# Attention's transposes moved from VectorE to the DMA engines, and the down/wo weight sums from VectorE to accumulating DMAs in DRAM

## The chip, the cores and the metric

The kernel runs on one core of one Trainium2 chip. Times are device microseconds (us). PE is TensorE, DVE is VectorE, ACT is ScalarE, POOL is GpSimd, SP is SyncE, which issues most of the DMAs. PEld is TensorE's loading of weights. A name with a q at the end (SPq, POOLq) is that engine's queue of instructions, which keeps the order that the program gave it. L335 is line 335 of that run's own kernel, so the same operation has other numbers in other runs. In an operation `out<-in` names the tiles; in a list of waits `a <- b` means that a waited for b.

## The reference, cut to what matters

```python
# x: 1 x 2048 x 1024 (bf16), wqkv: 1024 x 3072, wo: 1024 x 1024, w_gate and w_up: 1024 x 3584, w_down: 3584 x 1024
g = sigmoid((x * gate_w).sum(-1, keepdims=True))
a = attention(x @ wqkv) @ wo          # 32 heads of 32; each query sees 8 keys, at distances 0, 2, .. 14
b = (gelu(x @ w_gate) * (x @ w_up)) @ w_down
return g * a + (1 - g) * b
```

## The kernel before: the parts that matter

The 2,048 rows are handled as four chunks of 512. The gate/up products run twice (two passes of two chunks, 14 blocks of weights each), the down and wo products once per chunk. These products are done with seven half-size matrix products in place of eight, which needs sums and differences of weight blocks ("forms"). A program in Python lays out all instructions beforehand: every piece of work is an `Op` with an assumed cost, and the order on each engine is fixed by those costs. On the chip each engine then follows its fixed order and waits where data is late.

Three parts matter here. First, the forms of the gate/up weights. In the first pass they are made by VectorE from four loaded pieces and stored to DRAM from GpSimd's queue for the second pass. Pieces and forms live in a ring of 20 slots, and a form's slot is only free again when TensorE has used it **and** its store has landed:

```python
def wforms():                                   # per block of gate/up weights: four forms
    ...
    o = dve(t, go, [("w", 0, b, x_), ("w", 0, b, y_)], key=("w", 0, b, f), lag=0.5, pre=ring_pre)
    yield o
    ...
    yield Op("POOL", (P * GR * 2, 0.6),
             lambda b=b, f=f: nc.gpsimd.dma_start(out=fdram[b][:, f * GR:(f + 1) * GR], in_=ring[:, held[("w", 0, b, f)], :]),
             [("w", 0, b, f)], key=("ws", b, f))
# in the gate/up products, first pass, when a form has been used:
ring_give(("w", sup, b, form), o, w.done[("ws", b, form)])      # o: the matmul, ws: the store
```

Second, the forms of the down and wo weights. They are staged in SBUF, summed by VectorE and stored, all but one store of them before the gate/up pass begins at 93 us:

```python
def preps():                                    # nine steps
    f0 = dve(t, lambda: V(out=fo[:, 0], in0=b12, in1=b11, op=ALU.subtract), [("prep", i0)], lag=1.0)
    ...                                         # four such differences, then four 256 KB stores
    o = Op("POOL", ..., lambda f=f: nc.gpsimd.dma_start(out=dd[:, f, r0:r0 + n, :], in_=fo[:, f]), [last], ...)
```

Third, attention, in eight halves of a chunk. The products of queries and keys are turned by VectorE in blocks of 32 x 32, and the weights are turned back later:

```python
o = dve(2.24, taking("z", lambda: nc.vector.transpose(out=flat("z"), in_=xbuf[:, accs[h], :])), [("qk", h)], ...)
...
def back(i=i):
    nc.vector.transpose(out=flat("ab")[:, i * n // 2:(i + 1) * n // 2], in_=flat("e")[:, i * n // 2:(i + 1) * n // 2])
```

## Time and profile before

| | before |
|---|---|
| median, 3 runs | 733.29 us (732.34 to 733.42) |
| PE busy | 721.8 of 729.7 us (99%) |
| VectorE busy | 631.6 us (87%) |
| share of the 16 DMA engines, 8 to 50 us / 141 to 200 us | 1.09 / 0.72 |

Lines of the profile's page for the kernel before: span, busy time by engine, busy tenths in 40 equal slices, and the DMA queues (q1 is fed by SyncE, q0 by GpSimd; ScalarE has a queue of its own, q10, with 0.2%; the last figure is the share of the 16 engines' time).

```profile
span 729.7 us, 9971 instructions
...
PE 721.8 (99%) x3397; PEld 356.0 (49%) x3397; DVE 631.6 (87%) x935; ACT 314.9 (43%) x532; POOL 72.0 (10%) x128
...
PE   8999999999999999999999998999999999999998
...
DVE  2689999999999989999899999999999999969300
...
DMA  9999965648892869943029999555455544899992
...
q1 hardware_dynamic: 142624, 135.30, 60.1%
q0 software_dynamic: 8544, 27.27, 10.1%
```

TensorE is never idle for a slice. Here is whom it waited for, from the list of waits of before (total us, times, longest):

```profile
PE ps L970 <- ACT m L1024: 2.1, 1, 2.1
PE ps L279 <- DVE hT L277: 1.2, 1, 1.2
PE ps L1212 <- DMA hT<-in_A_x_dram: 0.8, 1, 0.8
```

So TensorE loses 4.1 us to waits in the whole program. VectorE is busy but not in its way.

### The profile page before, as it was taken

What the parts mean: (1) busy time and instruction counts of PE and PEld (TensorE: products, weight loads), DVE (VectorE), ACT (ScalarE), POOL (GpSimd) and SP (SyncE); (2) the same over time, 40 slices, a digit from 0 to 9 for tenths busy, and PEclk for the clock granted to TensorE, in tenths of its full rate; (3) what the DMA queues carried; (4) which work ended last, traced back from release to release, by engine and by line L of the source; (5) the groups of instructions that cost most, each with busy time, mean ns of one, the idle gap of its engine ahead of it and who ended that gap; (6) DMA issues with size and microseconds to landing.
All of it is one profiled execution on the core that took longest, in us unless ns stands there. A gap on an engine that the chain in (4) does not pass through costs nothing.

```text
span 729.7 us, 9971 instructions
## 1 busy us (share of the span) xinstructions
PE 721.8 (99%) x3397; PEld 356.0 (49%) x3397; DVE 631.6 (87%) x935; ACT 314.9 (43%) x532; POOL 72.0 (10%) x128
## 2 busy tenths in 40 slices
PE   8999999999999999999999998999999999999998
PEld 5666644444444444456665444444444444444443
DVE  2689999999999989999899999999999999969300
ACT  2333455558555561035652113576557654220110
POOL 2234422121210100000000001000000000001000
PEclk9999999999999999999999999999999999999999
DMA  9999965648892869943029999555455544899992
GB/s 302 333 325 363 380 200 170 187 139 212 213 227 74 280 194 326 314 162 116 29 89 300 358 302 333 165 150 155 147 159 147 156 151 145 303 304 336 323 303 104
DMA packets 151507, 163.73 MB, mean 224 GB/s; under 512 B 22944, under 2 KB 112032, under 8 KB 151456
## 3 DMA queue, kind: packets, MB, share of 16 engines
q1 hardware_dynamic: 142624, 135.30, 60.1%
q0 software_dynamic: 8544, 27.27, 10.1%
q8 instruction: 26, 0.43, 0.2%
q10 hardware_dynamic: 288, 0.52, 0.2%
q14 instruction: 25, 0.20, 0.1%
HBM read 129.50 MB, written 28.31 MB: 216 GB/s over the span
## 4 chain that ended last, share of the span: by engine, by line
PE 73%; issue 21%; DVE 2%; ACT 1%; DMA 1%; POOL 1%; POOLq 0%; ACTq 0%
PE ps L970 44%; PE ps L1117 17%; PE ps L473 11%; DVE xbuf L922 1%; POOL out_dram L1144 1%; DMA hT<-in_A_x_dram 0%; DVE xbuf L930 0%; PE ps L1212 0%; DMA out_dram<-ost 0%; DVE xbuf L935 0%; DVE ost L1191 0%; ACT ost L1152 0%; ACT L1058 0%; DVE xbuf L787 0%; PE ps L717 0%
## 5 line engine op out<-in xcount | busy, mean ns | idle before, releaser
L970 PEld LDWEIGHTS <-ring 128*128 128x128 bf16 x1568 | 153.2, 98 | 187.7 <-issue 3.5
L970 PE MATMUL ps<-lend,ring 128*128 128x512 bf16 x896 | 212.3, 379 | 2.2 <-ACT m L1024 2.1
L970 PE MATMUL ps<-tf,ring 128*128 128x512 bf16 x672 | 164.0, 379 | 0.0
L1117 PE MATMUL ps<-ring,hT 128*128 128x512 bf16 x708 | 160.7, 379 | 0.0
L1117 PEld LDWEIGHTS <-hT 128*128 128x128 bf16 x708 | 69.2, 98 | 83.3
L781 DVE TENSOR_TENSOR xbuf<-qo,lend 128x2048 bf16<-128x2048 bf16 x64 | 77.4, 1218 | 2.1 <-ACT lend L495 2.1
L922 DVE TENSOR_TENSOR xbuf<-xbuf,lend 128x2048 bf16<-128x2048 bf16 x64 | 77.4, 1218 | 0.1
L787 DVE TENSOR_TENSOR xbuf<-xbuf 128x2048 bf16<-128x2048 bf16 x56 | 68.2, 1218 | 0.2
L609 PEld LDWEIGHTS <-ring 128*128 128x128 bf16 x336 | 44.0, 131 | 28.7 <-DMA ring<-in_A_wqkv_dram 0.4
L473 PE MATMUL ps<-lend,ring 128*128 128x512 bf16 x256 | 56.3, 381 | 0.1
L1042 ACT ACTIVATE gl<-ps 128x512 bf16<-128x512 f32 x56 | 33.5, 598 | 51.5 <-PE ps L970 51.4
L999 ACT COPY ps<-ps 128x512 f32<-128x512 f32 x56 | 32.0, 571 | 54.9 <-PE ps L970 54.8
L1152 ACT ACTIVATE ost<-ps,omg 128x512 bf16<-128x512 f32 x16 | 11.0, 688 | 102.5 <-PE ps L1117 99.3
L1144 POOL DMA_DIRECT2D out_dram<-ost x24 | 13.0, 540 | 413.4 <-ACT ost L1152 319.4
L1117 PE MATMUL ps<-ring,qo 128*128 128x512 bf16 x192 | 49.3, 379 | 0.0
L473 PEld LDWEIGHTS <-ring 128*128 128x128 bf16 x256 | 36.8, 145 | 19.0 <-issue 0.7
L443 POOL DMA_DIRECT2D fforms<-ring x56 | 30.4, 544 | 132.4 <-DVE ring L435 120.6
L609 PE MATMUL ps<-lend,ring 128*128 128x512 bf16 x192 | 43.5, 379 | 0.0
L1014 DVE TENSOR_TENSOR hT<-hT,gl 128x1024 bf16<-128x1024 bf16 x56 | 38.4, 686 | 5.8 <-ACT hT L1011 4.5
L930 DVE TENSOR_TENSOR xbuf<-xbuf 128x1024 bf16<-128x1024 bf16 x64 | 41.9, 686 | 0.7
L1054 DVE TENSOR_TENSOR u<-ps,u 128x512 f32<-128x512 f32 x56 | 38.4, 686 | 4.6 <-PE ps L970 3.4
L1033 DVE TENSOR_TENSOR hT<-ps,m 128x512 bf16<-128x512 f32 x56 | 38.4, 686 | 4.0 <-PE ps L970 3.9
(106 smaller groups left out, 724.7 us busy)
## 6 DMA issues: line engine op xcount, KB each, us to landing
ring<-dforms SPq DMA_DIRECT2D x112, 256.0 KB, 4.9
ring<-in_B_w_down_dram SPq DMA_DIRECT2D x84, 256.0 KB, 4.1
ring<-in_B_w_gate_dram SPq DMA_DIRECT2D x56, 256.0 KB, 4.7
fforms<-ring POOLq DMA_DIRECT2D x56, 256.0 KB, 4.5
ring<-fforms SPq DMA_DIRECT2D x56, 256.0 KB, 3.9
ring<-in_B_w_up_dram SPq DMA_DIRECT2D x42, 256.0 KB, 3.3
ring<-in_A_wqkv_dram SPq DMA_DIRECT2D x40, 256.0 KB, 4.9
ring<-oforms SPq DMA_DIRECT2D x32, 256.0 KB, 5.6
```

Source lines behind the costliest of these rows:

```text
L473: nc.tensor.matmul(banks[bk][:], lhsT=lhsT, rhs=xT(c, kt), start=(kt == 0), stop=(kt == KT - 1))
L609: nc.tensor.matmul(banks[bk][:], lhsT=lhsT, rhs=rhs[:, kt, :], start=(start and kt == 0), stop=(kt == KH - 1), skip_group_check=True)
L781: V(out=w3(box[t]), in0=q_b, in1=k_w, op=ALU.mult)
L787: V(out=w3(box[0]), in0=w3(box[0]), in1=w3(box[t]), op=ALU.add)
L922: return dve(tt(n), taking(("p", t), lambda: V(out=w3(box["p", t]), in0=w3(box["ab"]), in1=v_w, op=ALU.mult)), [("qkv", c, 2, t), abo] + ( ...
L930: V(out=s4(t)[:, t % 2], in0=w3(box["p", t])[:, 0:4], in1=w3(box["p", t])[:, 4:8], op=ALU.add)
L970: nc.tensor.matmul(banks[bk][:], lhsT=wv[:, k, fl * P:(fl + 1) * P], rhs=rhs[:, k, :], start=(start and k == 0), stop=(k == KH - 1), skip_ ...
L1014: yield dve(tt(2 * SC), lambda f=f: nc.vector.tensor_tensor(out=hT[:, :, f, :], in0=hT[:, :, f, :], in1=gl[f][:].rearrange("p (j s) -> p j ...
L1033: ev[f, "up2"] = dve(tt(SC, True), lambda f=f: nc.vector.tensor_tensor(out=hs(f, 1), in0=v3(banks[Bk[f]][:]), in1=v3(m5[f][:]), op=ALU.add ...
L1042: nc.scalar.activation(out=gl[f][:, SC:2 * SC], in_=banks[A[f]][:], func=ACT.Gelu_apprx_tanh)
L1054: e = dve(tt(SC, True), lambda f=f: nc.vector.tensor_tensor(out=u2[f][:], in0=banks[Dk[f]][:], in1=u2[f][:], op=ALU.add), [o, ev[f, "u2"]])
L1117: nc.tensor.matmul(banks[bk][:], lhsT=l, rhs=wv[:, i, :], start=(start and k == 0), stop=(q == last and i == 1), skip_group_check=True)
```

## The change

The intent is to take about 65 us of work off VectorE and have it done by DMAs. 24 DMA transposes issued from SyncE replace the 24 VectorE transposes, and the sums of the down/wo weights become 64 DMAs from DRAM to DRAM issued from GpSimd, 32 of them accumulating. The accumulating DMAs used here only add, so some signs change further on (`S1` is now a difference, and so on). The loads of x for the second pass become a stream of their own. The core of the diff:

```diff
-        for i0 in range(0, NPREP, 2):
-            ...                                  # staged loads, four VectorE differences, four stores
+        def part(kind, k0, n):
+            ...
+            return [(src(0, 0), dst(0), None), (src(1, 1), dst(2), None), (src(1, 1), dst(1), None), (src(1, 0), dst(3), None),
+                    (src(0, 1), dst(0), ALU.add), (src(0, 1), dst(2), ALU.add), (dst(0), dst(1), ALU.add),
+                    (dst(1), dst(3), ALU.add)]
+        done, j = [("qkv", 0, 1, NT - 1)] * NFLY, 0          # NFLY = 2
+        for kind, k0, n in PARTS:                            # one part of wo (512 KB DMAs), seven of down (256 KB)
+            for src, dst, op in part(kind, k0, n):
+                def go(src=src, dst=dst, op=op):
+                    if op is None:
+                        nc.gpsimd.dma_start(out=dst, in_=src)
+                    else:
+                        nc.gpsimd.dma_start(out=dst, in_=src, accum_op=op, max_dma_last_dim=1024)
+                d = [done[-NFLY]]
+                if j >= NEARLY:                              # NEARLY = 28, PER = 3
+                    d.append(("w", 0, (j - NEARLY) // PER, 3))
+                o = Op("POOL", (n * P * NW * 2 * (2 if op else 1), 1.0), go, d, after=True)
 ...
-        o = dve(2.24, taking("z", lambda: nc.vector.transpose(out=flat("z"), in_=xbuf[:, accs[h], :])), [("qk", h)],
-                pre=xb_pre(), key=("acct", h))
+        def turn(cols, fn, deps, **kw):
+            return Op("SP", (P * cols * 2, max(1.3, cols / 1000.0)), fn, deps, tail=2.0 if h == 0 else 1.1, lag=1.0, **kw)
+        o = turn(n, taking("z", lambda: nc.sync.dma_start_transpose(out=rows("z"), in_=xbuf[:, accs[h], :])), [("qk", h)],
+                 pre=xb_pre(), key=("acct", h))
 ...
-                nc.vector.transpose(out=flat("ab")[:, i * n // 2:(i + 1) * n // 2],
-                                    in_=flat("e")[:, i * n // 2:(i + 1) * n // 2])
+                nc.sync.dma_start_transpose(out=rows("ab")[:, i * NWIN:(i + 1) * NWIN],
+                                            in_=flat("e")[:, i * n // 2:(i + 1) * n // 2])
```

Waits between sums that touch the same bytes are needed for the result; the limit of two sums in flight is the schedule's own choice. The Trainium skill, "DMA: Bandwidth & Descriptors" (Rules for kernel authors), says that an accumulate reads its destination and writes it later with nothing holding the bytes in between, and that one must wait for the earlier DMA's semaphore.

## The prediction

> **What bounds the kernel.** TensorE. The page's first part has PE busy 721.8 of 729.7 us (99%), clock 1.0 in every slice. The groups and timeline show one 128x512 matmul every 0.216 us; the 3,296 of the program need 712 us. The list of waits gives PE only 2.1 us on ScalarE near 456 us, 2.0 us at the start, and some 3.5 us of tail after the last matmul. VectorE is at 87%, but PE hardly waits for it. The DMA engines are saturated from 8 to 93 us (share 1.07) and the down products (0.89 to 0.99 from 275 to 320 us), half free (0.55) in the first gate/up pass.
>
> **What the change moves.** PE's work is unchanged, so nothing below about 727 us is possible.
> - VectorE loses 36 weight sums (0.685 us each, 24.7 us) and the 32x32 transposes (8 of 2.31 us, 16 of 1.23 us: 38.2 us) and small copies: about 65 of 632 us, nearly all off the critical path. At most the 2.1 us wait goes.
> - The sums become 64 DRAM-to-DRAM DMAs from GpSimd, half accumulating. The 36 staged loads and 36 stores (18.9 MB) go. The Trainium skill, "Collectives: The Full Stack" (bandwidth ceiling: AG, RS, AR), says an accumulate is slow because it needs two source reads. No run here shows that yet. Estimate from it: some 27 MB-equivalents, half of it in the gate/up pass.
> - 24 SBUF-to-SBUF DMA transposes (8 MB). The 16 x transposes between 177 and 213 us raise the DMA share by about 0.43 (15.5 us for 2 MB), so an estimate of 3.8 us of all engines per 512 KB and 62 us in total. In the gate/up pass the share goes from 0.55 to about 1.0.
>
> **Where it can hurt.**
> 1. The chain of sums: each waits for the one two before it. Its stores landed in 6.1 us (dforms) and 4.5 us (fforms). Estimate 5 to 6 us for a plain part, 7 to 8 for an accumulate: 64 x 6.5 / 2 = 208 us from about 50 us, ending near 258 us. The first summed weights are needed at about 265 us. So it just makes it, or is late by tens of us.
> 2. The fforms stores of the gate/up forms stand in the same GpSimd queue behind these waits. A late store holds a ring slot and delays the weight loads. There is some 30 us of slack.
> 3. Transposes wait in SyncE's queue while weight loads stand behind them. In the down products (0.87 us per piece, about 10 pieces ahead, landing 4.9 us) only 4 to 5 us are spare, and two halves of the attention fall in each of the stretches 270 to 320 and 400 to 440. I expect a few us of PE waits on ring DMAs there.
>
> **Prediction.** Either nothing is seen (730 to 738 us) or the chain is late and PE waits 15 to 40 us between 110 and 275 us. Median 739 us, range 730 to 772. Faster by over 2%: 0.01; within 2%: 0.58; slower: 0.41.
>
> **What would show it.** VectorE busy near 567 us. PE busy unchanged at 722 us. Accumulates landing later than plain parts, 7 to 8 us. The last dforms DMA issued between 225 and 265 us; if later, a PE wait on a ring<-dforms DMA just after 260 us. GpSimd's waits for sums appear ahead of fforms. Small PE waits for ring loads in the down products of chunks 0 and 1. Transposes land in 5 to 8 us.
>
> **What would make it wrong.** Accumulates far slower than a plain store (over 10 us): then the first pass is bound by the chain and the time goes over 780 us. Or accumulates as quick as plain ones: then 731 us.

## More of the kernel before

The windows of before, in the first gate/up pass and the start of the first down products; the first column is the stretch, then its length, busy time per engine, granted clock, DMA share and GB/s:

```profile
141.00:200.00 59.00, 58.98 (x274) 26.68 (x273) 57.56 (x83) 37.44 (x64) 10.80 (x20) 1.00 0.72 192
200.00:250.00 50.00, 50.00 (x234) 22.66 (x232) 47.84 (x66) 27.79 (x50) 6.49 (x12) 1.00 0.67 180
250.00:300.00 50.00, 50.00 (x233) 22.64 (x232) 46.92 (x71) 18.19 (x28) 1.62 (x3) 1.00 0.81 268
```

The DMA engines have room in these stretches (0.67 to 0.81).

## The result, and the profile after

The changed kernel took **763.64 us** (median of 4 runs, 760.4 to 769.96) against 732.82 us before (4 runs): a ratio of 1.0431, 95% interval 1.0351 to 1.0512. It is slower by over 4%. (Ratios here and below are the mean time of one kernel's fast runs over that of the other's of the same rounds, so not quite the ratio of the medians quoted.) The result is correct.

The same lines of the page, for the changed kernel:

```profile
span 765.1 us, 9884 instructions
...
PE 730.1 (95%) x3397; PEld 357.1 (47%) x3397; DVE 569.9 (74%) x842; ACT 313.9 (41%) x533; POOL 107.1 (14%) x156
...
PE   8999999968988859999999999999999999999998
...
DVE  1898799576877939938979897888999995694201
...
DMA  9797999999999994998212999997566656899993
...
q1 hardware_dynamic: 166368, 134.25, 61.9%
q0 software_dynamic: 18208, 36.71, 20.2%
```

VectorE did get its relief, 569.9 us in place of 631.6. TensorE has gaps from the ninth to the fifteenth slice, that is 153 to 287 us, the later part of the first gate/up pass. GpSimd's DMA queue q0 takes twice its share. TensorE's two large waits, from the list of waits of the changed kernel:

```profile
PE ps L964 <- DVE hT L1027: 15.9, 5, 9.5
PE ps L964 <- ACT m L1018: 13.0, 8, 3.4
```

And its windows, with columns as before:

```profile
141.00:200.00 59.00, 47.82 (x205) 20.52 (x204) 38.27 (x55) 22.79 (x42) 25.36 (x34) 0.94 0.90 219
200.00:250.00 50.00, 43.77 (x192) 18.93 (x191) 40.34 (x59) 23.62 (x44) 20.44 (x31) 0.97 1.14 258
250.00:300.00 50.00, 38.24 (x169) 16.70 (x167) 35.77 (x54) 23.81 (x41) 9.56 (x14) 0.90 0.97 219
```

The two large waits make 28.9 us, where before there was one of 2.1 us. PE's busy time also grew, by 8.3 us (730.1 against 721.8), for the same 3,397 matmuls. The granted clock in the windows tells why: 0.94, 0.97 and 0.90 in place of 1.00. The sum, 26.8 + 8.3 = 35.1 us, is nearly all of the difference of the two spans (765.1 - 729.7 = 35.4 us). The Trainium skill, "TensorE: Matmul & The Clock Gate" (Part 1), has it that the clock falls to half after an idle window of about 3.4 us and needs about as long to recover. This trace agrees in the main: after waits of 3.44 and 9.52 us (both below) the next eight matmuls took 3.57 and 3.39 us, where eight take 1.89 us at full clock, and full clock was back 5.9 and 3.0 us after they started. The limit is not sharp here: after one wait of 2.78 us eight matmuls took 3.23 us, after another of 2.84 us they took 1.89 us.

### One stall, followed back

A stretch of the timeline of the changed kernel: start, duration, engine, line, operation; in brackets the idle time before it and what ended it.

```profile
180.95 3.37 SPq L335 DMA_DIRECT2D ring<-in_B_w_gate_dram  x2
...
182.09 0.69 DVE L424 TENSOR_TENSOR ring<-ring 128x1024 bf16<-128x1024 bf16 x1 [4.71 <-DMA ring<-in_B_w_up_dram]
...
183.76 0.68 DVE L1048 TENSOR_TENSOR u<-ps,u 128x512 f32<-128x512 f32 x1
...
184.48 0.63 ACT L1052 ACTIVATE gl<-u 128x512 bf16<-128x512 f32 x1 [5.45 <-DVE u L1048]
...
185.48 0.59 ACT L1018 COPY m<-ps 128x512 f32<-128x512 f32 x1
...
186.12 3.57 PE L964 MATMUL ps<-lend,ring 128*128 128x512 bf16 x8 [3.44 <-ACT m L1018]
```

Read it from the bottom. TensorE idled 3.44 us for a ScalarE copy (L1018). ScalarE had to do the gelu (L1052) first in its order, and that waited 5.45 us for a VectorE add (L1048). VectorE had to make a weight form (L424) first in its order, and that waited 4.71 us for a weight piece that was late. Nothing here is short of engine time: one late load stops three in-order queues in turn.

Why was the load late? These are SyncE's own waits for stores of forms in the changed kernel, between 140 and 200 us and then over the whole run:

```profile
SPq L335 <- DMA fforms<-ring: 51.8, 11, 9.6
...
SPq L335 <- DMA fforms<-ring: 72.8, 17, 9.6
```

For 51.8 of 60 us SyncE stood before a weight load (L335) because the ring slot was still held by a store of a form (fforms<-ring). Before the change no such line exists. The stores were not slow to land once issued (5.2 to 8.6 us in this stretch); they were issued late, since they stand behind the sums in GpSimd's queue. GpSimd's waits for sums in the changed kernel:

```profile
POOL dforms L406 <- DMA dforms<-dforms: 41.1, 7, 7.6
POOL dforms L406 <- DMA dforms<-in_B_w_down_dram: 36.0, 15, 5.1
...
POOL dforms L404 <- DMA dforms<-in_B_w_down_dram: 23.4, 11, 5.1
...
POOL dforms L404 <- DMA dforms<-dforms: 16.1, 6, 4.5
```

These are 116.6 us of standing still in that queue. The line of 41.1 us holds a wait that the schedule did not foresee: it counts on two sums in flight, but the last accumulate of a part reads what the one just before it writes.

TensorE's longest wait, 9.5 of the 28.9 us, has another cause. It does not come from a weight load; what it goes back to is a DMA transpose (L907):

```profile
263.61 7.27 SPq L907 DMA_TRANSPOSE xbuf<-xbuf  x2
...
265.49 4.26 POOL L432 DMA_DIRECT2D fforms<-ring  x7
...
282.04 1.23 DVE L916 TENSOR_TENSOR xbuf<-xbuf,lend 128x2048 bf16<-128x2048 bf16 x1 [12.36 <-DMA xbuf<-xbuf]
...
283.79 0.68 DVE L1027 TENSOR_TENSOR hT<-ps,m 128x512 bf16<-128x512 f32 x1
...
284.52 3.39 PE L964 MATMUL ps<-tf,ring 128*128 128x512 bf16 x8 [9.52 <-DVE hT L1027]
```

VectorE stood 12.36 us before its attention work until the transpose had landed, and behind it in its order stood the operation (L1027) that TensorE needed. The transposes L907 took 5.6 us to land in the median, these two 17.3 and 14.1 us. While these two were being issued, GpSimd began to issue seven held-back stores in a row (256 KB each, from 265.5 us); that these delayed the transpose is a guess that no run tried.

### The profile page after: what moved, and what is told of

The parts are those of the page before. It is cut to its first block, busy times and chain, and to the rows that moved or that the text cites. A ratio compares the mean times of both kernels' runs of the same rounds, so it can differ in the third digit from the quotient of the medians.

```text
span 765.1 us, 9884 instructions
## 1 busy us (share of the span) xinstructions
PE 730.1 (95%) x3397; PEld 357.1 (47%) x3397; DVE 569.9 (74%) x842; ACT 313.9 (41%) x533; POOL 107.1 (14%) x156
## 3 DMA queue, kind: packets, MB, share of 16 engines
q0 software_dynamic: 18208, 36.71, 20.2%
## 4 chain that ended last, share of the span: by engine, by line
PE 68%; DMA 21%; issue 4%; DVE 2%; POOL 2%; ACT 2%; SPq 0%; POOLq 0%; DVEq 0%; ACTq 0%
PE ps L1111 28%; PE ps L964 26%; PE ps L598 9%; DMA dforms<-in_B_w_down_dram 6%; DMA dforms<-dforms 4%; PE ps L462 4%; DMA oforms<-in_A_wo_dram 2%; DMA ring<-in_B_w_up_dram 2%; DMA xbuf<-xbuf 2%; DMA oforms<-oforms 2%; DMA ring<-in_B_w_gate_dram 2%; POOL dforms L404 1%; DMA fforms<-ring 1%; DMA ring<-in_A_wo_dram 1%; POOL fforms L432 1%
## 5 line engine op out<-in xcount | busy, mean ns | idle before, releaser
L964 PEld LDWEIGHTS <-ring 128*128 128x128 bf16 x1568 | 154.5, 99 | 222.0 <-issue 42.8
L964 PE MATMUL ps<-lend,ring 128*128 128x512 bf16 x896 | 215.5, 383 | 13.2 <-ACT m L1018 13.0
L964 PE MATMUL ps<-tf,ring 128*128 128x512 bf16 x672 | 166.7, 384 | 16.1 <-DVE hT L1027 15.9
L1052 ACT ACTIVATE gl<-u 128x512 bf16<-128x512 f32 x56 | 35.4, 632 | 60.1 <-DVE u L1048 60.0
L424 DVE TENSOR_TENSOR ring<-ring 128x1024 bf16<-128x1024 bf16 x56 | 38.1, 687 | 29.4 <-DMA ring<-in_B_w_up_dram 18.0
L1048 DVE TENSOR_TENSOR u<-ps,u 128x512 f32<-128x512 f32 x56 | 38.4, 686 | 6.6 <-PE ps L964 6.0
```

Source lines behind the costliest of these rows:

```text
L424: nc.vector.tensor_tensor(out=g, in0=ring[:, held[("w", 0, b, x_)], :], in1=ring[:, held[("w", 0, b, y_)], :], op=op)
L964: nc.tensor.matmul(banks[bk][:], lhsT=wv[:, k, fl * P:(fl + 1) * P], rhs=rhs[:, k, :], start=(start and k == 0), stop=(k == KH - 1), skip_ ...
L1048: e = dve(tt(SC, True), lambda f=f: nc.vector.tensor_tensor(out=u2[f][:], in0=banks[Dk[f]][:], in1=u2[f][:], op=ALU.add), [o, ev[f, "u2"]])
L1052: ev[f, "g2"] = act(0.54, lambda f=f: nc.scalar.activation(out=gl[f][:, 0:SC], in_=u2[f][:], func=ACT.Gelu_apprx_tanh), [e], table="gelu")
```

## The experiments

Theories. **Queue**: sums stand in front of the stores in GpSimd's queue, slots come free late, weight loads come late. **Traffic**: the sums and transposes fill the DMA engines (share 0.90 to 1.14 between 141 and 250 us, where before it was about 0.7), and everything lands late, whoever issues it. **Transposes**: a late DMA transpose holds the in-order queues of VectorE or SyncE.

| label | what it is | median us | ratio to before | 95% interval |
|---|---|---|---|---|
| (changed kernel) | | 763.64 | 1.0431 | 1.0351 to 1.0512 |
| e1_dve_turns | sums by DMA, transposes on VectorE | 750.32 | 1.0248 | 1.0221 to 1.0276 |
| e2_dve_sums | transposes by DMA, sums on VectorE | 733.70 | 1.0019 | 0.9977 to 1.0060 |
| e3_stores_act | changed, stores of forms from ScalarE | 749.32 | 1.0229 | 1.0201 to 1.0258 |
| e4b_half | changed, sums move half the bytes (wrong result) | 733.61 | 1.0011 | 0.9981 to 1.0042 |
| e5_turns_stores | e1 and e3 together | 736.40 | 1.0055 | 1.0030 to 1.0080 |
| e6_plain | changed, no accumulating (wrong result) | 740.96 | 1.0118 | 1.0079 to 1.0157 |
| e7_pairs | changed, two parts interleaved | 753.48 | 1.0289 | 1.0245 to 1.0333 |
| e8_pairs_stores | e7 and e3 together | 751.50 | 1.0264 | 1.0246 to 1.0281 |
| e9_patient | e3, later landing of transposes foreseen | 752.95 | 1.0295 | 1.0273 to 1.0318 |
| e10_traffic | e5 and unused copies from SyncE | 741.62 | 1.0135 | 1.0115 to 1.0155 |
| e11_many | e10 with the copies cut in 128 KB DMAs | 753.54 | 1.0299 | 1.0253 to 1.0345 |

All but the two marked gave correct results. The kernel before had medians of 731.98 to 732.82 us in these rounds.

### Each half of the change alone: e1_dve_turns and e2_dve_sums

```diff
# e1: in the changed kernel, the transposes as before (and with them the layout of the gate's sums)
-        o = turn(n, taking("z", lambda: nc.sync.dma_start_transpose(...
+        o = dve(2.24, taking("z", lambda: nc.vector.transpose(...
# e2: in the changed kernel, load_prep() and preps() as before, with the new signs
-                        nc.gpsimd.dma_start(out=dst, in_=src, accum_op=op, max_dma_last_dim=1024)
+            f0 = dve(t, lambda: V(out=fo[:, 0], in0=b12, in1=b11, op=ALU.add), [("prep", i0)], lag=1.0)
```

> Undoes one half: the attention's transposes are back on VectorE as before, the accumulating sums stay. Queue theory (sums stand ahead of the forms' stores in GpSimd's queue, late stores hold ring slots, weight loads come late): most of the loss stays, 748 to 760 us, and SyncE's queue still waits over 40 us for the fforms stores. Transpose theory (a late DMA transpose holds VectorE's or SyncE's in-order queue): most of the loss goes, 733 to 740 us.

> Undoes the other half: the sums are back on VectorE with staged loads and stores, the DMA transposes stay. Queue theory: 732 to 740 us, no wait of SyncE's queue for fforms stores, PE waits under 6 us. Transpose theory: most of the loss stays, 750 us or more, with VectorE waiting for xbuf<-xbuf transposes.

The DMA transposes alone cost nothing that these runs can tell (1.0019, interval across 1), and VectorE waited 8.7 us for them in e2, where it waited 27.9 us in the changed kernel. The sums alone cost 2.5%. SyncE's wait for stores in e1, in its own queue's list:

```profile
SPq L336 <- DMA fforms<-ring: 66.8, 12, 14.7
```

That is close to the 72.8 us of the changed kernel. The transposes by themselves are out as the cause. But the two halves do not add up: 18 us and 2 us alone, 31 us together. Something that the sums do makes the transposes harmful.

### Taking the stores out from behind the sums: e3_stores_act and e5_turns_stores

```diff
-             lambda b=b, f=f: nc.gpsimd.dma_start(out=fdram[b]...
+             lambda b=b, f=f: nc.scalar.dma_start(out=fdram[b]...
```

The laying out of the program is left as it was, so TensorE, VectorE and SyncE keep their order.

> The changed kernel with the 56 stores of the gate/up forms issued from ScalarE instead of GpSimd; the order on PE, VectorE and SyncE is the same, the DMA work too. Queue theory: the stores land soon after their sums, SyncE's wait for fforms stores (72.8 us) falls below 20 us, time 738 to 750 us. Bandwidth theory (the DMA engines are full, whoever issues): no change, 757 to 768 us.

> Transposes back on VectorE (as e1_dve_turns, 750.3 us) and the forms' stores issued from ScalarE (as e3_stores_act, 749.3 us): only the accumulating sums are left on GpSimd, alone in its queue. If the sums alone hurt by their place ahead of the stores: 732 to 737 us. If they hurt by filling the DMA engines even without the transposes' traffic: 742 to 750 us.

SyncE's wait for stores fell from 72.8 us to 0.4 us in e3. Its only line for stores there:

```profile
SPq L907 <- DMA fforms<-ring: 0.4, 1, 0.4
```

The edit also moves the stores to another kind of DMA queue (q10, a hardware queue). That they land sooner once issued is not the reason: their median landing is 7.2 us in e3 and 7.7 us in the changed kernel. The time fell by 14.3 us in e3 (763.64 to 749.32) and by 13.9 us in e5 (750.32 to 736.40). The same edit is worth the same with and without the DMA transposes, so the queue part is shown, and it is some 14 of 31 us. This is what moving the stores was worth in all, for they now stand in ScalarE's order: at 228.0 and 238.6 us in e3 TensorE waited 2.95 and 2.85 us for a ScalarE copy that stood behind such a store. It is the larger part of what the sums cost alone (18 us). TensorE's waits in e5:

```profile
PE ps L961 <- ACT ps L990: 2.7, 3, 1.2
PE ps L961 <- ACT m L1015: 1.9, 2, 1.0
...
PE ps L961 <- ACT u L1041: 0.8, 1, 0.8
```

Some 0.55% (4 us) is left in e5, and 2.3% (17 us) in e3. The expected range for e3 (738 to 750 us) was met only just, at its upper end; the queue theory is not the whole.

e5 also answers the traffic theory in its plain form. Its windows, beside 0.90 and 1.14 in the changed kernel:

```profile
141.00:200.00 59.00, 59.00 (x275) 26.70 (x273) 54.80 (x78) 32.01 (x59) 14.80 (x16) 1.00 0.97 245
200.00:250.00 50.00, 46.28 (x212) 20.55 (x211) 45.15 (x72) 29.19 (x52) 9.93 (x11) 1.00 1.17 267
```

The DMA engines are as full as in the changed kernel, and the loss is 4 us.

### What a sum costs: e4b_half and e6_plain

```diff
# e4b: half of the rows of each part, and the loads of the forms read only what was written
-                return B_w_down[r0:r0 + n * P, ...]
+                return B_w_down[r0:r0 + n // HALF * P, ...]
# e6
-                        nc.gpsimd.dma_start(out=dst, in_=src, accum_op=op, max_dma_last_dim=1024)
+                        nc.gpsimd.dma_start(out=dst, in_=src)
```

> Wrong result on purpose: each of the 64 DMAs of the sums moves half its bytes, with the same number, order and waits. Bandwidth theory: the sums' DMA load halves, most of the loss goes, 735 to 747 us. Queue theory: a sum's latency is mostly fixed (5.8 us for 256 KB[...]), so the chain is hardly shorter: 750 to 762 us.

> Wrong result on purpose: the 32 accumulating DMAs are plain copies of the same bytes; orders on all engines unchanged. If the second read and the adding make the sums dear: these land in about 5.3 us (plain ones in the changed kernel) instead of 7.1 us, the software queue's share of the DMA engines falls from 20% to about 16%, time 738 to 752 us. If accumulating costs little: 757 to 768 us.

Half the bytes took away the whole loss, where I had expected the queue's part to stay: a miss. I had taken a sum's latency as mostly fixed. It was not: the median landing of accumulates fell from 7.2 to 5.3 us, that of the plain parts from 5.3 to 4.4, the last sum was issued at 225.6 us in place of 264.8, and no wait of SyncE for stores is left. So e4b relieves the queue and the engines at once and can't tell them apart. It does show that the amount moved by the sums is what sets both.

Without accumulating, with the same bytes written, the median landing of the DMAs in the accumulates' place fell from 7.2 to 5.4 us, SyncE's wait for stores from 72.8 to 32.4 us, and the time by 23 us. The share of the software queue in e6, beside 20.2% in the changed kernel:

```profile
q0 software_dynamic: 11072, 36.71, 15.9%
```

20.2% of 765.1 us is 155 us of all 16 engines, 15.9% of 737.3 us is 117 us: accumulating cost 37 us of DMA time in 32 DMAs that write 9.4 MB. The Trainium skill, "Collectives: The Full Stack" (The bandwidth ceiling), says of ReduceScatter that the adding is slow because two sources must be read. These runs agree in direction, but do not show that reason: the edit of e6 also takes away the limit on the length of a row (`max_dma_last_dim=1024`), and the 7,136 more packets of the changed kernel in this queue (18,208 against 11,072) may come from either.

### The chain's own length: e7_pairs and e8_pairs_stores

```diff
-        for kind, k0, n in PARTS:
-            for src, dst, op in part(kind, k0, n):
+        for i in range(0, len(PARTS), 2):           # step 0 of part A, step 0 of part B, step 1 of part A, ...
+            work_ += [s_ for step in zip(*pair) for s_ in step]
```

> The same 64 DMAs with two parts interleaved, so that the last accumulate of a part no longer waits for the landing of the one just before it, a wait that the schedule did not foresee (GpSimd waited 41 us for dforms<-dforms). All other orders are the same. Queue theory: the chain gets shorter, stores go earlier, 748 to 758 us. Bandwidth theory: 758 to 768 us.

> e7_pairs with the forms' stores issued from ScalarE. The stores do not stand behind the sums any more, so a quicker chain only raises the DMA load: 745 to 753 us, as e3_stores_act (749.3), if what is left there is DMA traffic delaying loads and transposes; under 742 us if it was the chain's own length.

With the stores behind the sums, the quicker chain gains 10 us (763.64 to 753.48), as the queue theory has it, though SyncE's wait for stores only fell to 60.6 us: that sum is no measure of the loss by itself. With the stores elsewhere it gains nothing (751.50 against 749.32). The length of the chain matters only through what stands behind it.

### What is left beside the queue: e9_patient, e10_traffic and e11_many

```diff
# e9, in e3
-            return Op("SP", ..., tail=2.0 if h == 0 else 1.1, lag=1.0, **kw)
+            return Op("SP", ..., tail=5.0, lag=1.0, **kw)
# e10, in e5: VectorE turns, and SyncE copies 1 MB, 512 KB, 512 KB into an unused DRAM buffer
+        yield copy(0, 8, [("qk", h)])
         o = dve(2.24, taking("z", lambda: nc.vector.transpose(...
# e11: the same copies as 8, 4 and 4 DMAs of 128 KB
```

> e3_stores_act (749.3 us) with a schedule that foresees a later landing of the DMA transposes (3.9 us more each), so that VectorE and SyncE have other work ahead of what waits for them; the DMA work is the same. If the rest of the loss is the wait of in-order queues for late transposes: under 743 us, and VectorE waits less for xbuf<-xbuf (29 us in e3_stores_act). If it is late weight loads behind full DMA engines: 745 to 755 us.

> e5_turns_stores (736.4 us; VectorE transposes, stores from ScalarE) with a plain DRAM-to-DRAM copy into an unused buffer issued from SyncE at each place of a DMA transpose, 2 MB per half of a chunk, which takes about as much of the DMA engines as its transposes (an estimate, 3.7 us per MB from e6_plain against 7.2 us per half). Nothing waits for the copies. If traffic alone makes the loss that the transposes add beside the sums: 744 to 755 us. If it is the wait for the transposes' results: 735 to 741 us.

> e10_traffic (741.6 us, ratio 1.0135) with each copy cut into DMAs of 128 KB: the same bytes, but SyncE is held about as long as by the transposes (8 issues of 0.55 us in place of one transpose of 4 to 5 us). Nothing waits for the copies' data; a later load may have to wait for a copy[...]. If the rest of what the transposes add (ratio 1.0229 in e3_stores_act) is their holding SyncE's queue: 745 to 752 us. If it is VectorE's wait for their results: 740 to 744 us.

Foreseeing late transposes did not help: the time rather went up, against the expectation of under 743 us if the wait for late transposes were the rest. VectorE's waits for xbuf<-xbuf fell from 29.2 us (e3) to 9.4 us (e9), and its waits for ring loads rose from 8.9 to 16.3 us. But the traces do not clear the transposes. In e3 TensorE's longest wait goes straight back to one, as in the changed kernel:

```profile
161.66 2.36 DVE L916 TENSOR_TENSOR xbuf<-xbuf,lend 128x2048 bf16<-128x2048 bf16 x2 [7.85 <-DMA xbuf<-xbuf]
...
165.28 3.57 PE L964 MATMUL ps<-tf,ring 128*128 128x512 bf16 x8 [6.02 <-DVE hT L1027]
```

In e9 TensorE's waits in the gate/up products (L964) fell from 14.8 us (e3) to 8.3 us. The wait for transposes that was left is a single one near 680 us, in the last down products; VectorE was busy from its end until it had made what TensorE then waited for. From the two engines' lists of waits in e9:

```profile
DVE xbuf L916 <- DMA xbuf<-xbuf: 9.4, 1, 9.4
...
PE ps L1111 <- DVE qo L933: 6.1, 2, 3.8
```

So e9 moved this wait more than it removed it, and it does not rule the wait out. (The profiled run of e9 is also its fastest, 748.57 us against a median of 752.95.)

Copies whose data nobody needs brought back part of it: e10 is at 1.0135 where e5 is at 1.0055 and e3 at 1.0229. The copies took 47 us of all engines by the share of the hardware queue (62.1% of 739.1 us less 56.1% of 734.1 us). The transposes took 67 us by the same reckoning of e3 against e5, and 56 us of e2 against before. So the traffic of e10 was too small to settle it alone.

The copies had another difference: their issue barely holds SyncE (though it waited 11.7 us in total because a later load had to wait for a copy). The copies' issues in SyncE's queue in e10 (count, then shortest, median and longest time of an issue in ns, first and last start):

```profile
L838 SPq DMA_DIRECT2D noise<-in_B_w_down_dram x24: 552/586/2554, 31.7 to 636.1; - x24
```

And the issues of the full-size transposes in e3:

```profile
L839 SPq DMA_TRANSPOSE xbuf<-xbuf x8: 1706/4922/8057, 44.9 to 614.9; - x8
```

An issue of a full transpose held SyncE 4.9 us, and weight loads stand behind it. This is not the sums' doing: in e2 the median was 4.1 us. SyncE also stood before the transposes until VectorE or ScalarE had made their input: 27 us between 93 and 290 us in e3, 21 us in e2. The copies have no such wait. In e11 the copies' bytes are the same as in e10, but the DMAs are 128, of 0.6 us each, so that SyncE is held about as long as by transposes. It took 753.54 us (1.0299), the whole of the loss of e3 and a little more, with no DMA transpose in attention at all. But e11 holds back more than SyncE's time of issue: SyncE waited 19.1 us in total for copies, and ScalarE, which issues the stores in this run, 9.6 us (5.4 and 4.2 us, none in e10); the wait of 5.4 us ended in one of TensorE's of 3.8 us. So "nothing waits for the copies" did not hold, and these ways are not told apart. What e11 shows is that a loss of this size can come without the results of transposes; it does not show that it came so in e3.

Nothing beat the kernel before: e2 comes within the noise of it, and with TensorE at 99% of the span before, no version of this change has more than 7.9 us, the idle time of TensorE, to win.

## Why the prediction was right or wrong

The time was inside the range (730 to 772 us), and the outcome was the slower of the two branches, which had been given 0.41, against 0.58 for no visible difference. The median of 739 us was 25 us too low. That the time fell inside the range is in part luck. The slower branch was drawn for a late chain, and TensorE's waits came to 28.9 us as drawn there (15 to 40 us), but from two other sources: stores behind the chain, and a transpose that landed late. Point by point:

- **TensorE bounds, VectorE's relief is worth nothing.** Right: VectorE fell to 569.9 us (567 predicted), and e2, where it lost 37 us with the transposes, is at 1.0019.
- **Cost of the sums.** Right in size: plain parts landed in 5.3 us (5 to 6 predicted), accumulates in 7.1 (7 to 8). The last sum was issued at 264.8 us (225 to 265 predicted), and the summed weights came in time: no wait of TensorE for them.
- **Stores behind the sums, "some 30 us of slack".** This is the step that failed: the mechanism was named, but taken as covered by the ring, so its term in the sum was nothing. The waits on stores were 72.8 us in SyncE's queue, and moving the stores gave 14 us back (e3, and again e5). The slack was an estimate of how long one slot may be held; my reading, argued and not tried by itself, is that the stores were late from block to block, so that the slack was used up once and not regained.
- **Transposes ahead of the loads.** Predicted as a few us in the down products. There TensorE waited 0.2 us. The harm came in the gate/up pass, where DMA share was about 1 as predicted, and only beside the sums: some 13 us (e3 against e5, and the changed kernel against e1). The prediction counted the hold on SyncE's queue but not VectorE's wait for a landing; it had landings of 5 to 8 us, and the two that made the 9.5 us stall took 17.3 and 14.1 us. e10 has 5 us for copies of two thirds to five sixths of the DMA time; how the rest divides between the hold on SyncE and waits for results stays open.
- **"PE busy unchanged at 722 us".** Wrong: 730.1 us. The sum left out that the clock falls after a long wait. The waits of 28.9 us (15 to 40 predicted) thus cost 35 us.

Of the 31 us, then: about 14 from the stores' place in the queue, about 4 from the sums otherwise, about 13 from the transposes beside the sums (by which of their ways is not shown). All of it hangs on the amount of DMA work that the sums bring (e4b).

## What to carry to other kernels

Work taken off an engine that nobody waits for gains nothing, and put on the DMA engines it can cost: look at what is already in the queue that will issue it, and at what stands behind it. A chain of waits should not share an in-order queue with stores that free buffers; once the slack of the buffers is used up, every late store becomes a late load. Count for each DMA both its share of the engines and the time that its issue holds the queue, and treat a TensorE wait of about 3 us or more as dearer than its length (2.78 us was enough here once, and 2.84 us was not another time). Look at the longest wait first, not at a typical one: here they had different causes.

## What the Trainium skill lacked or had wrong

- "Advanced Engine Details and Errata" (X-Bar Transpose) says that transpose DMAs are as fast as regular DMAs. Here 24 SBUF-to-SBUF transposes (8.4 MB) took 56 us of all 16 engines (e2 against before), 6.7 us per MB, where plain DRAM-to-DRAM copies took 2.8 us per MB (e10 against e5, 47 us for 16.8 MB). No plain SBUF-to-SBUF copy was run beside them.
- "DMA: Bandwidth & Descriptors" gives the issue of transposes only as cycle counts in a part on trn3 B0, with earlier generations beside it. The time that one SBUF-to-SBUF transpose holds the issuing queue here: 4.1 us median for 128 x 2048 (e2), 1.5 us for 128 x 1024, against 0.59 us for a plain copy of 512 KB to 1 MB (e10).
- No page has a time for an accumulating DMA within DRAM: 7.1 us from issue to landing for 256 KB, 5.3 us for a plain one, and 1.17 us against 0.70 us of GpSimd's time to issue it. The issue of the stores from the same queue also went from 0.54 to 1.00 us, and back to 0.56 us in e6 without accumulating; why was not tried.
